# A new emission order for the first third of a fused gated long-convolution and mixer kernel

## The chip, the cores and the metric

The kernel runs on one core of a Trainium2 chip. Its time is the device time of one execution in microseconds (us). Five engines work side by side, each through its own list of instructions in order: TensorE (PE) with matmuls and transposes, VectorE (DVE) and ScalarE (ACT) with element-wise work and with emptying PSUM, GpSimd (POOL) with small work and the gathers of V, and SyncE (SP), which asks for nearly all transfers. Semaphores tie the lists together. Since every list is in order, an instruction that waits holds up all behind it on its engine.

## The reference

```python
x = A_q                                              # 2048 tokens x 640 channels, bf16
g = sigmoid((x * gate_w).sum(-1, keepdims=True))
# a: shifted k times v, then a causal convolution over all 2048 tokens per channel, by FFT
k_shift = sum over t<4 of shift(k, t) * shift_k[:, t];  kv = k_shift * v
y = irfft(rfft(pad(kv)) * rfft(pad(ssm_k)))[:2048] + kv * ssm_D
a = x * y
# b: a token-shift MLP and a second MLP, both with a layernorm ahead and a residual
h  = gelu(layernorm(x) @ w1)                         # 640 x 640
hs = concat(h's four groups of 160 channels, shifted by +1, -1, +2, -2 tokens) @ w2
x1 = x + hs
b  = x1 + gelu(layernorm(x1) @ w3) @ w4              # 640 x 1536, 1536 x 640
out = g * a + (1 - g) * b
```

## The kernel before

The whole program is written as small *steps*, and one string, `ORDER`, lists all 1101 of them. A step is named `what.arguments:number`, for example `mlp1.1.4:0`; the loop `emit` calls them one by one, and each call puts its instructions at the end of the lists of its engines. So the order of every engine is the order of that string, and nothing reorders it. A string of letters among the arguments (`VAAV`) says for each part of a step whether DVE (V) or ACT (A) empties its PSUM tile. A second table, `SLOTS`, gives each temporary its buffer: `c` the eight PSUM banks, `row` four SBUF buffers of 128x2560 that hold K chunks (`kn`), normalised rows (`xn`) and the rows `stg` on their way to DRAM, `gt` and `gq` smaller ones. A buffer is reused when its last reader is done, so a new tile can wait for an emptying, or for a transfer, several steps back.

The tokens are cut as token = 16p + t, with p the partition and t in 0..15 (`NT`), so a chunk `c` of four t's holds 512 tokens. The first third of the program ("the head" below) does this:

- `warm` issues 23 matmuls on zeros. `load_x0`, `load_x`, `k_load:0`, `load_w1`, `load_w2`, `load_h`, `load_gw` ask SP for x, K, W1, W2, the convolution kernel (`E`, `E4`) and the gate's weights; `v_load` asks POOL to gather V.
- `x_stats`, `x_norm`, `x_turn` take the layernorm of chunk c and transpose it. Chunks 0 and 1 are turned on PE (into `xt`), chunks 2 and 3 by a transposing transfer on SP's queue (`x_turn.3.D`, `x_turn.2.D`, line 653; tile `xt`).
- `mlp1.c.u` is one of 20 groups of five matmuls with W1 (tile `WN`; u=4 takes the mixed columns `WM`) and a gelu into `HT`. `h_shift` copies shifted channels of `HT` into `HM` on POOL.
- `k_load` transposes K on PE into `KT`; `k_wrap` and `kv_consts` prepare `KW` and `DG`; `tap.k` (k=0..4) is the 4-tap convolution for 128 channels, 76 small matmuls into four PSUM banks, each then multiplied by V in place in `KV` (line 606 from PSUM, or line 600 on ACT and then 603 on DVE).
- `step1.KV.c` is the first stage of the Fourier transform of `KV`: five pairs of matmuls, ten emptyings into `stg`, two sends to DRAM (`S_x`). `step1.HT0.c` does the same for the convolution kernel, which `h_transpose` has turned (`S_h`).
- `w2.t` multiplies row t of the shifted h by W2 (tile `WP`), adds x on DVE and sums squares on ACT. `z_rows` and `z_cols` are the gate's matmuls; `z_rows:0` spreads the gate's weights (`GWR<-GW`) on POOL. `t2_table` and `i_tables` make the twiddle factors; `t2_table:1` has a POOL instruction of 128x1024 integers (line 322).

After the head come the rest of `w2`, `step1.HT0`, the second MLP (`w3`, line 841; `w4`, line 868), the second and third Fourier stages (`step2`, `product`, `step3`), `step4` and the stores.

Of the kernel before, what the change touches and what calls it, by code (L numbers as in the profile page):

```python
# [41 lines left out]
def kernel(  # L42
# [837 lines left out]
    def step4(t1, ev):  # L880
# [53 lines left out]
        "x_stats.0.VVVA:4 "
        "x_stats.0.VVVA:5 "
        "x_stats.0.VVVA:6 "
        "warm:4 "
        "row_order:0 "
        "k_load.2.VAV:0 "
        "f1_table:0 "  # L940
        "x_norm.0.VVAA:0 "
        "x_norm.0.VVAA:1 "
        "f4_table:1 "
        "x_stats.1.VVVV:0 "
        "k_load.3.AVA:2 "
        "load_x.3:0 "
        "x_norm.0.VVAA:2 "
        "x_stats.1.VVVV:1 "
        "k_load.3.AVA:3 "
        "x_turn.0.AAA:0 "  # L950
        "k_load.3.AVA:6 "
        "k_load.2.VAV:5 "
        "load_w1.1:0 "
        "x_norm.0.VVAA:3 "
        "k_load.2.VAV:1 "
        "x_stats.1.VVVV:2 "
        "x_turn.0.AAA:1 "
        "x_stats.1.VVVV:3 "
        "x_turn.0.AAA:2 "
        "x_stats.1.VVVV:4 "  # L960
        "load_w1.0:0 "
        "x_stats.1.VVVV:5 "
        "x_stats.3.VVAA:0 "
        "k_load.3.AVA:4 "
        "x_norm.1.VVVV:0 "
        "x_turn.0.AAA:4 "
        "k_load.2.VAV:3 "
        "x_turn.0.AAA:3 "
        "x_turn.0.AAA:5 "
        "x_stats.3.VVAA:1 "  # L970
        "x_norm.1.VVVV:1 "
        "x_norm.1.VVVV:2 "
        "v_load.2:0 "
        "k_load.0.AAV:0 "
        "f1_table:1 "
        "mlp1.0.2:0 "
        "mlp1.0.3:0 "
        "x_norm.1.VVVV:3 "
        "v_load.0:0 "
        "k_load.1.AVV:0 "  # L980
        "k_load.2.VAV:6 "
        "mlp1.0.0:0 "
        "load_x.2:0 "
        "x_stats.3.VVAA:2 "
        "x_turn.1.VVV:0 "
        "x_turn.1.VVV:4 "
        "mlp1.0.1:0 "
        "x_stats.3.VVAA:3 "
        "x_turn.1.VVV:1 "
        "k_load.2.VAV:4 "  # L990
        "x_stats.3.VVAA:4 "
        "x_stats.3.VVAA:5 "
        "k_load.0.AAV:3 "
        "x_turn.1.VVV:5 "
        "mlp1.0.3:1 "
        "x_stats.3.VVAA:6 "
        "x_turn.1.VVV:2 "
        "v_load.3:0 "
        "x_turn.1.VVV:3 "
        "k_load.1.AVV:3 "  # L1000
        "w1_mixed:0 "
        "v_load.1:0 "
        "mlp1.0.0:1 "
        "x_stats.2.VVAA:0 "
        "mlp1.0.2:1 "
        "k_load.0.AAV:1 "
        "mlp1.0.1:1 "
        "x_stats.3.VVAA:7 "
        "k_load.0.AAV:5 "
        "mlp1.1.2:0 "  # L1010
        "x_norm.3.VVVV:0 "
        "x_norm.3.VVVV:1 "
        "k_load.0.AAV:4 "
        "load_cj:0 "
        "k_load.0.AAV:2 "
        "mlp1.1.2:1 "
        "x_norm.3.VVVV:2 "
        "x_norm.3.VVVV:3 "
        "x_stats.2.VVAA:1 "
        "k_load.1.AVV:5 "  # L1020
        "mlp1.0.4:0 "
        "k_load.1.AVV:4 "
        "mlp1.0.4:1 "
        "k_load.1.AVV:1 "
        "d_fold:0 "
        "mlp1.1.4:0 "
        "x_turn.3.D:0 "
        "kv_consts:0 "
        "x_stats.2.VVAA:2 "
        "mlp1.1.0:0 "  # L1030
        "k_load.2.VAV:2 "
        "k_wrap:0 "
        "k_load.1.AVV:6 "
        "mlp1.1.4:1 "
        "k_load.0.AAV:6 "
        "x_stats.2.VVAA:3 "
        "t2_table:0 "
        "load_w2:0 "
        "mlp1.1.3:0 "
        "k_load.1.AVV:2 "  # L1040
        "tap.3.VAVA:0 "
        "mlp1.1.0:1 "
        "x_stats.2.VVAA:4 "
        "h_shift.1:0 "
        "mlp1.1.3:1 "
        "tap.4.VAAV:0 "
        "x_stats.2.VVAA:5 "
        "tap.3.VAVA:1 "
        "tap.3.VAVA:3 "
        "tap.3.VAVA:5 "  # L1050
        "h_shift.0:0 "
        "mlp1.1.1:0 "
        "tap.4.VAAV:7 "
        "x_stats.2.VVAA:6 "
        "tap.3.VAVA:4 "
        "tap.4.VAAV:1 "
        "load_h.2:0 "
        "tap.3.VAVA:7 "
        "z_cols:0 "
        "mlp1.1.1:1 "  # L1060
        "load_gw:0 "
        "tap.4.VAAV:5 "
        "tap.4.VAAV:3 "
        "mlp1.3.1:0 "
        "tap.3.VAVA:2 "
        "x_stats.2.VVAA:7 "
        "x_norm.2.AVVV:0 "
        "mlp1.3.1:1 "
        "mlp1.3.4:0 "
        "tap.4.VAAV:2 "  # L1070
        "mlp1.3.0:0 "
        "x_norm.2.AVVV:1 "
        "tap.4.VAAV:8 "
        "x_norm.2.AVVV:2 "
        "x_norm.2.AVVV:3 "
        "h_shift.0:1 "
        "tap.4.VAAV:6 "
        "tap.3.VAVA:6 "
        "mlp1.3.4:1 "
        "tap.4.VAAV:4 "  # L1080
        "mlp1.3.0:1 "
        "tap.2.AVAA:0 "
        "x_turn.2.D:0 "
        "h_shift.3:0 "
        "tap.0.AVAA:0 "
        "tap.2.AVAA:3 "
        "tap.2.AVAA:7 "
        "tap.2.AVAA:5 "
        "tap.3.VAVA:8 "
        "mlp1.3.3:0 "  # L1090
        "tap.0.AVAA:3 "
        "h_shift.0:2 "
        "tap.0.AVAA:5 "
        "tap.2.AVAA:8 "
        "h_shift.3:1 "
        "mlp1.3.2:0 "
        "tap.0.AVAA:4 "
        "tap.2.AVAA:6 "
        "tap.0.AVAA:1 "
        "mlp1.3.3:1 "  # L1100
        "tap.0.AVAA:6 "
        "tap.1.VAVA:0 "
        "tap.0.AVAA:7 "
        "tap.1.VAVA:5 "
        "tap.1.VAVA:1 "
        "tap.2.AVAA:4 "
# [961 lines left out]
```

## Time and profile before

| what | us |
|---|---|
| three timed runs | 226.66, 231.12, 231.19 (median 231.12) |
| the profiled execution | 229.4 |
| its span, first to last instruction | 227.6 |
| busy: PE, DVE, ACT, POOL | 217.3, 185.1, 171.6, 37.8 |

The span is 1.8 us shorter than the execution's own time, for what lies before the first and after the last instruction. PE is busy for 95% of the span, and the profile counts an instruction as busy from its start to its modelled end, so the gaps that are left are few; they lie mostly in the first 45 us. The granted TensorE clock is 1.00 throughout.

### The profile page before, as it was taken

Reading aid. Unit: us, or ns where it says so; the run is one execution under the profiler, and the core shown is the slowest. Engines: PE = TensorE matmul, PEld = TensorE weight load, DVE = VectorE, ACT = ScalarE, POOL = GpSimd, SP = SyncE. Lnnn points to the kernel's source line nnn. Section 1 sums busy time; section 2 is a strip of 40 time slices with the busy share of each in tenths; the row PEclk is TensorE's granted clock in tenths of the full one; section 3 lists DMA queues with packets and bytes.
Section 4 is the critical chain, followed back from the end, with each engine's and each line's share of the span. In section 5 each row is a group of like instructions: output and inputs, shape, how many; then the busy total and the mean of one; then the engine's idle time right before and its main releaser. Section 6 shows DMA issues by size and latency. Waiting matters only on the chain.

```text
span 227.6 us, 6057 instructions
## 1 busy us (share of the span) xinstructions
PE 217.3 (95%) x2428; PEld 121.4 (53%) x2428; DVE 185.1 (81%) x447; ACT 171.6 (75%) x341; POOL 37.8 (17%) x91
## 2 busy tenths in 40 slices
PE   8989988799999997999999999999999999999994
PEld 3647545337855553334665544555533547657762
DVE  7999996977889968981899997989999941439994
ACT  4999986869899978999987597976989450266450
POOL 4247247806000331300510000000000000000000
PEclk9999999999999999999999999999999999999999
DMA  6999999888999899997799590593694779418915
GB/s 247 398 386 306 265 259 162 256 340 292 384 350 411 285 206 287 347 397 232 252 147 370 134 260 17 127 334 121 78 313 172 234 264 365 196 29 322 319 75 183
DMA packets 41802, 57.61 MB, mean 253 GB/s; under 512 B 18478, under 2 KB 34478, under 8 KB 41518
## 3 DMA queue, kind: packets, MB, share of 16 engines
q1 hardware_dynamic: 41198, 54.60, 76.8%
q0 software_dynamic: 576, 2.62, 3.3%
q8 instruction: 19, 0.31, 0.6%
q14 instruction: 9, 0.07, 0.1%
HBM read 34.93 MB, written 18.35 MB: 234 GB/s over the span
## 4 chain that ended last, share of the span: by engine, by line
PE 73%; ACT 14%; DMA 6%; DVE 4%; issue 1%; ACTq 0%
PE ps L868 23%; PE ps L841 22%; PE psm L708 5%; PE psw L789 5%; PE ps L466 4%; PE ps L894 4%; ACT stg L361 4%; DMA S_h<-stg 3%; PE ps L513 3%; PE ps L424 2%; ACT HT L711 2%; PE pst L391 2%; DMA S_x<-stg 2%; ACT KT L361 1%; PE psk L591 1%
## 5 line engine op out<-in xcount | busy, mean ns | idle before, releaser
L841 PE MATMUL ps<-x1t,W 128*128 128x512 bf16 x240 | 56.1, 380 | 0.1
L868 PEld LDWEIGHTS <-gt 128*128 128x128 bf16 x384 | 36.2, 98 | 17.8 <-issue 3.0
L845 ACT ACTIVATE gt<-ps 128x512 bf16<-128x512 f32 x48 | 27.6, 609 | 19.0 <-PE ps L868 10.6
L841 PEld LDWEIGHTS <-W 128*128 128x128 bf16 x240 | 21.8, 98 | 28.2 <-issue 5.5
L361 ACT CAST stg<-ps 128x512 bf16<-128x512 f32 x55 | 28.8, 608 | 5.3 <-PE ps L424 3.4
L868 PE MATMUL ps<-W4a,gt 128*128 128x320 bf16 (+2 forms) x160 | 27.1, 300 | 0.0
L868 PE MATMUL ps<-W4b,gt 128*128 128x320 bf16 (+2 forms) x160 | 27.0, 300 | 0.0
L871 DVE SCALAR_TENSOR_TENSOR X<-ps,OMG,X 128x320 bf16<-128x320 f32 (+2 forms) x32 | 17.2, 547 | 11.9 <-PE ps L868 11.7
L789 PE MATMUL psw<-WP,HT 128*128 128x320 bf16 x116 | 21.4, 300 | 1.3 <-ACT stg L361 1.3
L361 ACT CAST gs<-ps 128x320 bf16<-128x320 f32 x41 | 15.6, 440 | 8.8 <-PE ps L513 4.8
L708 PE MATMUL psm<-xt,WN 128*128 128x512 bf16 x80 | 19.1, 380 | 1.8 <-ACT xt L361 0.9
L363 DVE CAST XS<-ps 128x512 bf16<-128x512 f32 x19 | 12.5, 685 | 6.9 <-PE ps L466 6.9
L363 DVE CAST stg<-ps 128x512 bf16<-128x512 f32 x25 | 15.9, 684 | 2.1 <-PE ps L424 2.1
L361 ACT CAST hs<-ps 128x512 bf16<-128x512 f32 x28 | 15.0, 605 | 1.4 <-PE ps L466 1.4
L792 DVE SCALAR_TENSOR_TENSOR X<-psw,X 128x320 bf16<-128x320 f32 x32 | 14.5, 487 | 1.7 <-PE psw L789 1.5
L789 PEld LDWEIGHTS <-HT 128*128 128x128 bf16 x116 | 10.7, 98 | 8.1 <-issue 4.4
L898 ACT ACTIVATE y<-ps,GS 128x320 bf16<-128x320 f32 x22 | 10.4, 526 | 5.7 <-PE ps L894 3.5
L711 ACT ACTIVATE HT<-psm 128x512 bf16<-128x512 f32 x20 | 11.9, 616 | 3.1 <-PE psm L708 2.9
L868 PE MATMUL ps<-W4c,gt 128*128 128x320 bf16 (+2 forms) x64 | 13.9, 299 | 0.0
L708 PEld LDWEIGHTS <-WN 128*128 128x128 bf16 x80 | 7.5, 97 | 10.7 <-issue 1.3
L363 DVE CAST gs<-ps 128x320 bf16<-128x320 f32 x23 | 10.7, 485 | 2.4 <-PE ps L513 1.7
L789 PE MATMUL psw<-WP,HM 128*128 128x320 bf16 x44 | 12.3, 299 | 0.0
(155 smaller groups left out, 378.1 us busy)
## 6 DMA issues: line engine op xcount, KB each, us to landing
S_x<-stg SPq DMA_DIRECT2D x8, 640.0 KB, 4.3
S_h<-stg SPq DMA_DIRECT2D x8, 640.0 KB, 6.5
ax<-S_x SPq DMA_DIRECT2D x8, 640.0 KB, 7.8
ax<-S_h SPq DMA_DIRECT2D x8, 640.0 KB, 5.8
S_g<-gs SPq DMA_DIRECT2D x8, 640.0 KB, 3.5
kn<-in_A_k_dram SPq DMA_DIRECT2D x4, 640.0 KB, 5.0
E<-in_A_ssm_k_dram SPq DMA_DIRECT2D x5, 512.0 KB, 7.0
q<-in_A_q_dram SPq DMA_DIRECT2D x4, 640.0 KB, 4.6
```

Source lines behind the costliest of these rows:

```text
L361: A.copy(out=dst, in_=src)
L363: V.tensor_copy(out=dst, in_=src)
L466: PE.matmul(ps[j][q:q + 32, lo - 512 * u:hi - 512 * u], lhsT=CMP[HALF[j], 8 * b + 4 * h + i, c, :], rhs=st[name, 2 * b + h][HALF[j], i, lo ...
L708: PE.matmul(ps[:].rearrange("p (a b) -> p a b", a=4), lhsT=W1N[:, k, 160 * u:160 * u + P] if u < 4 else W1M[:, k, :], rhs=xt[:, :, k, :], ...
L711: A.activation(out=st["HT"][:, 4 * c:4 * c + 4, u, :], in_=ps[:].rearrange("p (t b) -> p t b", t=4), func=ACT.Gelu_apprx_tanh)
L789: PE.matmul(ps[:], lhsT=h_tile(f, t1), rhs=W2P[:, f, o:o + W], start=(f == 0), stop=(f == 4))
L792: V.scalar_tensor_tensor(out=X1[:, t1, o:o + W], in0=box["ps"][:], scalar=1.0, in1=X[:, t1, o:o + W], op0=ALU.mult, op1=ALU.add, accum_out ...
L841: PE.matmul(ps[:].rearrange("p (a b) -> p a b", a=4), lhsT=st["W3"][:, k, f * P:(f + 1) * P], rhs=xt[:, :, k, :], start=(k == 0), stop=(k ...
L845: A.activation(out=st["gt", c, f // 4][:, f % 4, :], in_=ps[:], func=ACT.Gelu_apprx_tanh)
L868: PE.matmul(ps[:], lhsT=st["gt", c, f // 4][:, f % 4, i * P:(i + 1) * P], rhs=st["W4", f // DC][:, f % DC, o:o + w], start=(f == 0), stop= ...
L871: V.scalar_tensor_tensor(out=X1[:, t1, o:o + w], in0=box["ps"][:], scalar=OMG[:, t1:t1 + 1], in1=X1[:, t1, o:o + w], op0=ALU.mult, op1=ALU ...
L898: A.activation(out=box["y"][:], in_=box["ps"][:], func=ACT.Copy, scale=GS[:, t1:t1 + 1])
```

## The change

The first 341 names of `ORDER` are written anew; from `w2.1:2` on (entry 341, counted from 0) the string is the same, except for one argument: `step1.KV.0` has other emptying letters. Every step of the head is still there once. What differs is their order, the letters (`tap.0` is `VVVA` and was `AVAA`, for example), and `SLOTS`, whose rows `c`, `row`, `gt` and `gq` are written anew for the whole program. Two places of the diff:

```diff
     SLOTS = {
-        "c": "012345670124703510347205142356401723605162370514731057423671045261304732641374153670421350627413"
+        "c": "012345670567401372605436057243610723014763024167503642167304521673251607426013572460157234603521"
...
-        "row": "01230213021302320123012031203120310310303",
+        "row": "01230123012323103210321302130213023023030",
...
     ORDER = (
-        "open.L1.left:0 "
-        "open.A2.right:0 "
-        "consts0:0 "
-        "load_x0.0:0 "
-        "warm:0 "
...
+        "open.L1.left:0 open.A2.right:0 consts0:0 warm:0 warm:1 warm:2 warm:3 warm:4 load_x0.0:0 consts0:1 "
...
+        "h_shift.1:0 h_shift.1:1 h_shift.1:2 load_w2:0 x_norm.3.VVVV:0 h_shift.1:3 x_norm.3.VVVV:1 x_norm.3.VVVV:2 "
+        "x_norm.3.VVVV:3 x_stats.2.VVAA:0 x_stats.2.VVAA:1 x_stats.2.VVAA:2 x_turn.3.D:0 x_stats.2.VVAA:3 "
+        "load_h.3:0 x_stats.2.VVAA:4 x_stats.2.VVAA:5 tap.4.VAAV:7 load_h.0:0 mlp1.1.3:0 tap.3.VVVA:7 tap.3.VVVA:6 "
```

SP's list of transfers, from the eighth entry on, before (`DMA_TRANSPOSE` are `x_turn.3` and `x_turn.2`, `WP` is W2, `E` the convolution kernel, `E_1123` its last 128 channels, `S_x<-stg` the sends of `step1.KV`):

```order
L564 DMA kn<-in_A_k_dram 128x2560 x2
L190 DMA X<-in_A_q_dram 128x2560
...
L653 DMA_TRANSPOSE xt_506<-xn 128x20x128
L207 DMA WP<-in_B_w_dram 128x4x640
L208 DMA WP<-in_B_w_dram 128x1x640
L183 DMA E<-in_A_ssm_k_dram 128x2048
L200 DMA GW<-in_gate_w_dram 128x5x1
L653 DMA_TRANSPOSE xt_506<-xn 128x20x128
L183 DMA E<-in_A_ssm_k_dram 128x2048 x2
L187 DMA E_1123<-in_A_ssm_k_dram 128x2048
L187 DMA E_1123<-in_A_ssm_k_dram 128x2032
L183 DMA E<-in_A_ssm_k_dram 128x2048
```

and the same stretch after the change:

```order
L190 DMA X<-in_A_q_dram 128x2560
L207 DMA WP<-in_B_w_dram 128x4x640
L208 DMA WP<-in_B_w_dram 128x1x640
L653 DMA_TRANSPOSE xt_701<-xn 128x20x128
L183 DMA E<-in_A_ssm_k_dram 128x2048 x3
...
L653 DMA_TRANSPOSE xt_701<-xn 128x20x128
L187 DMA E_1032<-in_A_ssm_k_dram 128x2048
L187 DMA E_1032<-in_A_ssm_k_dram 128x2032
L200 DMA GW<-in_gate_w_dram 128x5x1
L183 DMA E<-in_A_ssm_k_dram 128x2048
L438 DMA S_x<-stg 128x2560 x2
```

W2 has moved ahead of the first transposing transfer; three rows of `E` stand between the two transposing transfers, where W2, one row of `E` and the gate's weights stood; the last three rows and the gate's weights now come right ahead of the first sends.

DVE's list just ahead of and behind `x_norm.3` (the four `xn` in a row), before:

```order
L686 BN_STATS b_435<-X 128x6 x2
L687 BN_AGGR mv<-b_435 128x2
L665 TENSOR_SCALAR xn<-X,RS,NB 128x640 x4
L363 COPY KT<-pst 128x1024
L553 TENSOR_REDUCE i_509<-IDB 128x32
L554 TENSOR_TENSOR DG<-i_509,cr 128x640
L363 COPY KT<-pst 128x1024
L571 MEMSET KW 128x15
L572 COPY KW<-KT 128x15x64
L573 COPY KW<-KT 128x15x63
```

and after:

```order
L571 MEMSET KW 128x15
L572 COPY KW<-KT 128x15x64
L573 COPY KW<-KT 128x15x63
L363 COPY xt<-pst 128x512
L363 COPY xt<-pst 128x1024
L553 TENSOR_REDUCE i_494<-IDB 128x32
L554 TENSOR_TENSOR DG<-i_494,cr 128x640
L665 TENSOR_SCALAR xn<-X,RS,NB 128x640 x4
L686 BN_STATS b_694<-X 128x6 x2
L687 BN_AGGR mv<-b_694 128x2
L606 TENSOR_TENSOR KV<-psk,KV 128x16x32 x4
```

The preparation for the taps (`KW`, `DG`) has moved ahead of `x_norm.3`, and a pair of statistics of chunk 2 behind it.

On PE, all 23 warm matmuls now come first, where they were dealt out among the first K transposes; the first MLP's groups begin after 76 transposes of K and x instead of 60; the taps come one at a time with one to three `mlp1` groups between them (4, 3, 2, 1, 0), where two pairs (3 with 4, 2 with 0) and then tap 1 stood; and two halves of `w2` (rows 2 and 1) come before the gate's `z_rows`. `t2_table:1` moves from the last tap to a place behind the h_transposes.

More of the change, by code (lines that the diff above doesn't have):

```diff
@@ L934 @@
[L934 to L1106, printed above, removed]
-        "mlp1.3.2:1 "
-        "load_h.1:0 "
-        "mlp1.2.2:0 "
-        "tap.0.AVAA:8 "
-        "tap.2.AVAA:1 "
-        "tap.1.VAVA:7 "
-        "h_shift.1:1 "
-        "tap.0.AVAA:2 "
-        "load_h.3:0 "
```

926 lines of the change are left out of this document (6 added, 920 removed), and 165 rows, old and new, of the table ORDER.

## The prediction

> **What bounds the kernel now.** I read the windows first, cut where the new order ends. Columns are the stretch in us, its length, and the busy time of each engine with its count.
>
> ```profile
> 0.00:25.00 25.00, 22.85 (x180) 13.45 (x181) 22.58 (x87) 21.57 (x37) 10.32 (x25) 1.00 0.94 338
> 25.00:45.00 20.00, 17.03 (x432) 9.44 (x431) 17.88 (x46) 16.66 (x33) 13.16 (x31) 1.00 0.95 219
> 45.00:65.00 20.00, 19.54 (x190) 12.38 (x190) 16.14 (x39) 15.99 (x28) 3.62 (x7) 1.00 0.90 331
> 65.00:85.00 20.00, 20.00 (x147) 11.57 (x146) 16.70 (x58) 18.57 (x40) 4.18 (x8) 1.00 1.09 321
> 97.00:227.00 130.00, 127.26 (x1385) 69.97 (x1383) 100.95 (x190) 87.78 (x186) 3.70 (x11) 1.00 0.69 216
> ```
>
> The first number behind the length is PE: it is full from 65 us to the end but for a few us. In the first 65 us it is busy for 22.85 + 17.03 + 19.54 = 59.4 us, so it idles 5.6 us. That is all a new head can win directly, since PE's work in the head does not change. Then PE's waits up to 100 us (total, times, longest), and the chain of work that ended last around the place where the two orders meet:
>
> ```profile
> PE ps L424 <- DVE KV L603: 1.5, 1, 1.5
> PE psw L789 <- ACT stg L361: 1.3, 1, 1.3
> PE psz L229 <- DVE NPI L249: 1.0, 1, 1.0
> PE psm L708 <- ACT xt L361: 0.9, 1, 0.9
> PE psk L591 <- issue: 0.8, 1, 0.8
> ```
> ```profile
> 66.79 1.46 PE psw L789 x10
> 68.25 0.75 PE ps L424 x6
> ```
>
> The ten matmuls at 66.79 are `w2.1:2` and `w2.11:0`, the first of the kept order. I call 66.79 the meeting point. Behind it every engine does the same work in the same order, so I let a shift of the meeting point pass to the end one for one. The sum is then an account of PE's gaps before that point: those of the new order against 5.6 us.
>
> **What goes.** The 1.5 us wait is the last tap. Here DVE and POOL stand in each other's way:
>
> ```profile
> 43.12 1.91 POOL L322 TENSOR_TENSOR n<-ab 128x1024 int32<-128x1024 int32 x1
> 43.31 2.00 DVE L603 TENSOR_TENSOR KV<-yk,KV 128x512 bf16<-128x512 bf16 x1
> L603 DVE TENSOR_TENSOR KV<-yk,KV x12: 409/485/1997, 30.3 to 43.3; 128x512 bf16<-128x512 bf16 x12
> ```
>
> A product of the same shape takes 0.41 us at the least (the last row: shortest, median and longest of the twelve, in ns); it took 2.00 beside POOL's 1.91. In the new order that POOL instruction runs beside casts from PSUM, long after the taps, so this wait goes, and with it the 0.8 and 0.9 us ones, whose places no longer exist. All are inside the 5.6.
>
> **What comes, 1: the opening.** Warm matmuls first:
>
> ```profile
> 0.98 6.73 PE L229 MATMUL psz<-WZ 128*128 128x512 bf16 x20 [0.98 <-DVE NPI L249]
> 8.24 0.81 PE L229 MATMUL psz<-WZ 128*128 128x512 bf16 x3
> 6.29 1.28 ACT L278 ACT_TABLE_LOAD   x1
> 8.70 0.20 POOL L659 TENSOR_TENSOR NB<-MU,RS 128x4 f32<-128x4 f32 x1
> 10.40 0.93 ACT L663 ACTIVATE xn<-X,NB,RS 128x640 bf16<-128x640 bf16 x1
> ```
>
> 20 in 6.6 us and 3 in 0.6, so PE is free at 8.2 and turns K chunk 1 (20 transposes) until 9.4. `x_turn.0` now waits for ACT: three of the four rows are normalised there (`AAAV`), 0.82 us each from about 8.95, when POOL has the scale (8.70 and 0.20), as before. Row 1 is there at 10.6, row 2 at 11.4. With K transposes between, PE loses about 1.4 us; with the start 2.4. Bounds 0.5 (ACT drops a table load it had at 6.29 and may be earlier) to 2.0.
>
> **What comes, 2: the first transposing transfer.** Prices of PE's groups, from the chain: 12 transposes 0.67, three `mlp1` 3.40, a tap 1.09, 48 transposes of `E` 3.17, three pairs of `step1` 0.75.
>
> ```profile
> 16.86 0.67 PE pst L620 x12
> 31.67 3.40 PE psm L708 x15
> 40.26 1.09 PE psk L591 x76
> 58.33 3.17 PE pst L391 x48
> 57.57 0.75 PE ps L424 x6
> ```
>
> Up to `mlp1.3.4`, the first user of chunk 3, the new list has the warm-up (to 8.2), 120 transposes (7.0, at 0.67 for 12 as K's are), 10 `mlp1` (11.3), 3 taps (3.3) and the 1.4 above: PE arrives at 31.2. The data wait for `x_norm.3` on DVE, then for the transfer:
>
> ```profile
> 22.07 1.52 DVE L665 TENSOR_SCALAR xn<-X,RS,NB 128x640 bf16<-128x640 bf16 x4 [0.19 <-POOL NB L659]
> 24.10 0.36 DVE L553 TENSOR_REDUCE i<-IDB 128x32 bf16<-128x128 bf16 x1
> 24.49 0.83 DVE L554 TENSOR_TENSOR DG<-i,cr 128x640 bf16<-128x640 bf16 x1
> 25.86 0.41 DVE L572 COPY KW<-KT 128x960 bf16<-128x960 bf16 x1
> 26.18 0.80 DVE L573 COPY KW<-KT 128x945 bf16<-128x945 bf16 x1
> 23.61 4.46 SPq L653 DMA_TRANSPOSE xt<-xn  x1
> 34.04 3.98 SPq L653 DMA_TRANSPOSE xt<-xn  x1
> DMA to landing us min/median/max: 8.0/8.0/8.0
> ```
>
> DVE is busy almost throughout the first 25 us, so what is put ahead of `x_norm.3` delays it: `DG` (24.10 to 25.25: 1.15), `KW` (25.86 to 26.91: 1.05), two K copies of 1024 and one of 512 (0.6 and 0.35 each as they follow one another); taken away are a pair of statistics (1.0), one normalised row (1.52 for four: 0.4) and 0.25 of x copies. Net +2.1, less the 0.19 idle: end at 25.5 instead of 23.6. The landing of 8.0 us makes 33.5, a wait of 2.3. Bounds: 1.7 if DVE loses no time at hand-offs, 2.9 if W2's 0.8 MB, now ahead of V's gather, holds the rings 0.6 us longer. The early W2 itself gains nothing: its first user was at 52.25 and would be at about 48.
>
> **What comes, 3: the second one.** `x_norm.2` ends on DVE at about 34.4 (four tap products, the statistics and a pair of scales more ahead, fewer behind), much as before (34.04). From 33.5, PE has five `mlp1`, two taps and five pairs, 9.1 us, and wants chunk 2 at 42.6; 34.4 + 8.0 = 42.4 would do. But three rows of `E`, 1.57 MB, stand ahead in SP's queue, asked for behind the first transposing transfer. That what is asked for later lands later on this queue shows in a tiny one:
>
> ```profile
> 29.99 0.82 SPq L200 DMA_DIRECT2D GW<-in_gate_w_dram  x1
> GW<-in_gate_w_dram SPq DMA_DIRECT2D x1, 1.2 KB, 7.1
> 25.00:30.00 5.00, 4.57 (x163) 2.93 (x162) 4.86 (x20) 5.00 (x12) 1.55 (x3) 1.00 1.12 197
> 30.00:35.00 5.00, 4.37 (x20) 1.67 (x18) 4.97 (x14) 3.68 (x7) 2.95 (x8) 1.00 0.86 245
> 35.00:40.00 5.00, 4.23 (x163) 2.84 (x162) 3.22 (x7) 3.53 (x7) 4.08 (x14) 1.00 1.00 177
> ```
>
> 1.2 KB needed 7.1 us, to 37.1, behind W2 and a row of `E`; the transposing transfer behind it landed at 42.0, 4.9 us on. At 245 GB/s (last column, the stretch in which plain loads moved) three rows take 6.4 us from 33.5, and 4.9 more make 44.8: a wait of 2.2. At 197 it is 3.8; if the rings share freely, 0. I take 2.2, the stretch with the same kind of load.
>
> [...]
>
> **What comes, 4: sends of `KV`.** `step1.KV.2` reuses the buffers of `KV.1`, so its emptyings wait until those rows have landed:
>
> ```profile
> 49.35 4.28 DMA S_x<-stg
> 53.71 3.03 ACT L361 CAST stg<-ps 128x512 bf16<-128x512 f32 x6 [0.21 <-DMA S_x<-stg]
> ```
>
> Before, this cost ACT 0.21 us. In the new order the last three rows of `E` and the gate's weights, 1.56 MB, are asked for just ahead. From 44.8 they take 4.7 us at the 331 GB/s of the third window, the two sends 2.0 each: landed at 53.5, cast at 54.0. PE reaches `KV.2:6`, which needs those two banks, at 44.8 + 7.9 = 52.7. A wait of 1.3; bounds 0.2 (as before) and 2.7 (at the 219 GB/s of the second window).
>
> The two `w2` halves ahead of `z_rows` need `HM` from POOL by 48 and it is there by 43; their cost is nothing as long as POOL is that far ahead, else up to 1 us. `SLOTS` I cost at nothing: the banks I followed were all emptied before their next user came, but for those named.
>
> **Sum.** 2.4 + 2.3 + 2.2 + 1.3 = 8.2 against 5.6: 2.6 us later at the meeting point. On the profiled execution, 227.6 of span and 1.8 around it, that is 229.4 + 2.6 = **232.0 us**, 1.1% more; beside the median of the runs shown (231.12, of which the profiled one is 1.7 under) it is 0.4% more. 2% is about what a measurement of this kernel can tell from no change. By the bounds: 1.5 + 1.7 + 0 + 0.2 = 3.4 gives 227.2; 3.0 + 2.9 + 3.8 + 2.7 = 12.4 gives 236.2.
>
> **Rivals.**
>
> *Faster.* No transfer is late: the rings take the rows of `E` in time and the gaps are the 3.4 of the lower bounds, a gain of 2.2. ACT reaches the meeting point less loaded (one table load of 1.28 fewer), its sends of `HT0` start earlier, and the 1.3 us wait of `w2` for `stg` in the second list goes too: 229.4 - 3.5 = 225.9. For it: the losses of before have named causes and the new order removes them. Against: 34.4 + 8.0 has 0.2 us to spare, and any backlog uses that up. 0.26.
>
> *Slower.* The queue of SP runs at the pace that a transposing transfer leaves it, 177 GB/s. Three rows then take 8.9 us, chunk 2 lands at 47.3 (wait 4.7), and the rows behind it move the sends to about 59, where PE wants them at 55.2: with the casts a wait of 4.8. Gaps 2.4 + 2.3 + 4.7 + 4.8 = 14.2, 8.6 more than before; half a us may be regained at 85: 237.5. It decides below some 200 GB/s. For it: the 35 to 40 row; against: 331 GB/s in the next window. 0.32.
>
> *Nothing happens.* The gaps change place and stay 5.6: 229.4. It needs both transposing transfers at or below 2 us of wait and free sends. 0.08.
>
> The forecast has 0.34, and its own range is 227.2 to 236.2. Faster by over 2% has 0.26, within 2% 0.42 (the forecast and the rival in which nothing happens), slower by over 2% 0.32. The range, reaching into both other cases, is 224.5 to 238.5.
>
> **What would show it.** In the new profile: one tap product of 2.00 us gone; PE waiting near 31 us for `mlp1.3.4` by 2.3, near 43 us for `mlp1.2.4` by about 2, near 53 us in `step1.KV.2` for casts that wait for `S_x`; the landing of the second transposing transfer over 10 us; `w2.1:2` at 69.4. It is wrong if the second `xt` lands within 8 us, if PE is the last to arrive at chunk 3, or if the shift at 69 is not the shift at the end.

## The result, and the profile after

| kernel | median us | runs | range us |
|---|---|---|---|
| before | 227.5 | 8 | 226.66 to 231.19 |
| after the change | 232.63 | 8 | 232.15 to 233.38 |

The ratio is 1.0242, with a 95% interval of 1.022 to 1.0264: the new order is 2.4% slower. It counts only fast runs: two of the eight of before (231.12 and 231.19) are slow ones, and the median of the other six is 227.1. The time lies in the predicted range and 0.6 us above the predicted 232.0, but "within 2%", which had the most chance, did not happen. Two numbers have to be kept apart. The profiled execution of before took 229.4 us, 1.9 more than the median of its eight runs; that of after took 232.64, its median. So the two traces show 3.3 us (spans 227.6 and 230.9) of the 5.1 between the medians. What the quicker executions of before do better is not shown.

The windows of after, cut as those of before (PE's busy time is the first number behind the length):

```profile
0.00:25.00 25.00, 21.13 (x169) 12.39 (x170) 20.93 (x84) 19.61 (x32) 10.44 (x25) 1.00 0.92 311
25.00:45.00 20.00, 17.67 (x433) 9.69 (x432) 17.30 (x39) 16.38 (x33) 11.90 (x30) 1.00 0.92 248
45.00:65.00 20.00, 18.43 (x162) 9.87 (x159) 15.41 (x35) 15.17 (x27) 5.16 (x7) 1.00 0.78 265
97.00:227.00 130.00, 129.99 (x1438) 71.13 (x1438) 102.96 (x196) 91.01 (x193) 5.89 (x18) 1.00 0.69 219
```

PE idles 3.9 us in the first window (2.2 before) and 1.6 in the third (0.5 before). The last transposes of `E` and the meeting point `w2.1:2`, in PE's timeline of after:

```profile
65.78 1.24 PE L391 MATMUL pst<-IDB,E 128*128 128x128 bf16 x16
70.93 0.43 PE L789 MATMUL psw<-WP,HT 128*128 128x320 bf16 x2
```

The meeting point is at 70.93 in this view. In the same view of before it is at 66.72 (the chain in the prediction has 66.79), so it is 4.2 later. At the end 3.3 are left: the wait of 1.3 us of `w2` for `stg` near 85 us has gone. The seven largest of PE's waits of after up to 100 us:

```profile
PE pst L620 <- DMA kn<-in_A_k_dram: 1.6, 1, 1.6
PE ps L424 <- ACT stg L361: 1.3, 1, 1.3
PE psz L229 <- DVE NPI L249: 1.0, 1, 1.0
PE psm L708 <- DVE KV L606: 0.8, 1, 0.8
PE pst L620 <- ACT xn L663: 0.7, 2, 0.4
PE psk L591 <- ACT yk L600: 0.7, 1, 0.7
PE psk L591 <- DVE KV L606: 0.4, 1, 0.4
```

There is no wait for `xt<-xn`, the transposing transfers, on which 4.5 us of my sum rested. Instead there are waits for the tap products (`KV`, `yk`), which I had not named at all. The chain of work that ended last says why:

```profile
2.58 9.31 DMA X<-in_A_q_dram
...
16.38 1.02 POOL RS L658
...
22.02 9.53 DMA KV<-in_A_v_dram,ROWS
...
31.70 0.51 POOL HM L762
...
36.80 1.07 POOL RS L658
...
38.17 1.24 DVE xn L665 x3
...
50.94 4.83 DMA S_x<-stg
```

Read from the top: x's chunk 1, now fifth in SP's list, lands at 11.9; its statistics keep DVE until 16.3; POOL forms its scale at 16.38 and only behind that asks for V, from 17.87 to 22.02; the last V lands at 31.6. The gathers in before and in after (issue, count, duration, first and last start; then issue to landing):

```profile
L173 POOL DMA_INDIRECT KV<-in_A_v_dram,ROWS x4: 937/938/1220, 15.6 to 19.7; - x4
DMA to landing us min/median/max: 6.4/6.8/7.6
```
```profile
L173 POOL DMA_INDIRECT KV<-in_A_v_dram,ROWS x4: 937/1012/1221, 17.9 to 22.0; - x4
DMA to landing us min/median/max: 8.9/9.1/9.5
```

V is asked for 2.4 us later and needs 1.9 more: 31.6 instead of 27.3. Before, that left 3 us until the first tap product at 30.3. Now DVE and POOL both start at the landing:

```profile
31.68 2.48 DVE L606 TENSOR_TENSOR KV<-psk,KV 128x512 bf16<-128x512 f32 x4 [2.32 <-PE psm L708]
31.70 0.49 POOL L762 COPY HM<-HT 32x384 bf16<-32x384 bf16 x1 [4.91 <-DMA KV<-in_A_v_dram,ROWS]
34.22 0.38 PE L591 MATMUL psk<-DG,KT 32*128 32x128 bf16 x13 [0.37 <-DVE KV L606]
37.48 0.62 PE L591 MATMUL psk<-DG,KT 32*128 32x128 bf16 x16
41.27 0.38 PE L591 MATMUL psk<-DG,KT 32*128 32x128 bf16 x13 [0.67 <-ACT yk L600]
```

DVE's wait is put down to PE's matmul of that moment, but POOL's copy beside it names the gathers, and the second profile below names them for DVE too. From there to 45.9 DVE works off the products of the taps, with statistics, scales and normalised rows between them and one pause of 0.25 us, and the last three taps on PE wait for their banks: from their first to their last instruction they take 1.68, 1.30 and 2.26 us, 5.2 together where the tap of before shown above took 1.09, so 2.0 too much. Only half of that appears as waits (0.37 and 0.67). The rest is inside rows counted as busy, like the one at 37.48, whose sixteen matmuls took 0.40 in an unhindered tap.

### The profile page after: what moved, and what is told of

It reads as the page before. It is cut to its first block, busy times and chain, and to the rows that moved or that the text cites. A ratio compares the mean times of both kernels' runs of the same rounds, so it can differ in the third digit from the quotient of the medians.

```text
span 230.9 us, 6058 instructions
## 1 busy us (share of the span) xinstructions
PE 219.6 (95%) x2428; PEld 121.6 (53%) x2428; DVE 185.3 (80%) x447; ACT 172.0 (75%) x337; POOL 38.2 (17%) x91
## 4 chain that ended last, share of the span: by engine, by line
PE 71%; DMA 10%; DVE 8%; POOL 5%; issue 2%; ACT 1%; SPq 1%; POOLq 0%; ACTq 0%; DVEq 0%
PE ps L841 23%; PE ps L868 23%; PE psw L789 6%; PE ps L466 5%; DMA KV<-in_A_v_dram,ROWS 4%; DMA X<-in_A_q_dram 4%; PE ps L894 4%; PE ps L424 3%; PE ps L513 3%; PE pst L391 2%; DVE X L792 2%; DMA S_x<-stg 2%; POOL HM L762 2%; PE psm L708 1%; POOL KV L173 1%
## 5 line engine op out<-in xcount | busy, mean ns | idle before, releaser
L841 PEld LDWEIGHTS <-W 128*128 128x128 bf16 x240 | 21.9, 98 | 28.6 <-issue 5.9
L361 ACT CAST stg<-ps 128x512 bf16<-128x512 f32 x50 | 27.0, 597 | 5.0 <-PE ps L424 2.7
L871 DVE SCALAR_TENSOR_TENSOR X<-ps,OMG,X 128x320 bf16<-128x320 f32 (+2 forms) x32 | 17.2, 548 | 11.9 <-PE ps L868 11.7
L363 DVE CAST stg<-ps 128x512 bf16<-128x512 f32 x30 | 19.2, 683 | 3.0 <-PE ps L424 2.9
L708 PEld LDWEIGHTS <-WN 128*128 128x128 bf16 x80 | 7.3, 97 | 11.9 <-issue 4.4
L363 DVE CAST gs<-ps 128x320 bf16<-128x320 f32 x23 | 10.7, 484 | 2.4 <-PE ps L513 1.7
L798 ACT ACTIVATE jk<-X 128x640 bf16<-128x640 bf16 x16 | 12.1, 757 | 0.5 <-DVE X L792 0.4
```

Of the source, the lines that this page charges most:

```text
L361: A.copy(out=dst, in_=src)
L363: V.tensor_copy(out=dst, in_=src)
L708: PE.matmul(ps[:].rearrange("p (a b) -> p a b", a=4), lhsT=W1N[:, k, 160 * u:160 * u + P] if u < 4 else W1M[:, k, :], rhs=xt[:, :, k, :], ...
L798: A.activation(out=jk[:], in_=X1[:, t1, :], func=ACT.Square, accum_out=S12[:, 1, t1:t1 + 1])
L841: PE.matmul(ps[:].rearrange("p (a b) -> p a b", a=4), lhsT=st["W3"][:, k, f * P:(f + 1) * P], rhs=xt[:, :, k, :], start=(k == 0), stop=(k ...
L871: V.scalar_tensor_tensor(out=X1[:, t1, o:o + w], in0=box["ps"][:], scalar=OMG[:, t1:t1 + 1], in1=X1[:, t1, o:o + w], op0=ALU.mult, op1=ALU ...
```

## The experiments

All times are medians in us. The kernel before ran in every call too, and its own median moved between calls (226.98 to 228.9). So two kernels are compared by their ratios within one call, and the mechanism by the traces. The ratio is the middle of its interval, not the quotient of the two medians beside it.

| kernel | us | before in that call | ratio | 95% interval |
|---|---|---|---|---|
| after_again | 232.04 | 226.98 | 1.022 | 1.0192 to 1.0248 |
| x3_dve | 233.13 | 226.98 | 1.0264 | 1.0232 to 1.0296 |
| before_w2_early | 233.48 | 226.98 | 1.0294 | 1.0268 to 1.0321 |
| v_first | 236.11 | 228.9 | 1.0278 | 1.0197 to 1.036 |
| w2_back | 232.05 | 228.9 | 1.0143 | 1.0063 to 1.0223 |
| e_back | 236.31 | 228.9 | 1.032 | 1.0248 to 1.0392 |
| x3_last | 232.01 | 228.9 | 1.0127 | 1.0057 to 1.0196 |
| opening | 232.75 | 228.45 | 1.0153 | 1.0066 to 1.024 |
| sx_free | 231.74 | 228.45 | 1.0131 | 1.0052 to 1.0211 |
| combo | 237.19 | 228.45 | 1.0357 | 1.0275 to 1.0439 |
| before_x3_first | 229.72 | 228.45 | 1.0032 | 0.9998 to 1.0065 |
| before_t2_late | 228.41 | 228.48 | 1.001 | 0.9979 to 1.0041 |

One thing stays open for the single repairs w2_back, x3_last, opening and sx_free. By ratio (1.0127 to 1.0153) they lie 0.7 to 1.2 points under the changed kernel (1.022 and 1.0242). By median (231.74 to 232.75) they lie within 0.9 us of it (232.04 and 232.63). The changed kernel was not run in their calls. These were on chip 3, where before took 228.45 and 228.9; after_again was on chip 5, where it took 226.98. So it isn't shown whether the repairs gained or before was only slower there.

### The changed kernel again

> The changed kernel as it is, in one call with the next two, so that they stand against it on one chip and not only against the kernel before. Its ratio was 1.024; the runs of single repairs lay at 1.013 to 1.015 although their traces reach the meeting point no sooner. If the ratio belongs to the change, 1.022 to 1.026 again; if the chip matters, 1.013 to 1.018. The wait for the first K chunk at 9 us, there in two of three profiles of this opening, is expected at 1.4 to 1.8 us.

It measured 1.022: the loss is there in this call too. In the profile mlp1 starts at 16.02, 0.66 us sooner than in the first one, and yet the last transposes of `E` end at 67.02 in both. The reason is in DVE's timeline:

```profile
31.64 1.89 DVE L606 TENSOR_TENSOR KV<-psk,KV 128x512 bf16<-128x512 f32 x3 [2.93 <-DMA KV<-in_A_v_dram,ROWS]
```

The first product waits 2.9 us for V and starts where it started before. So those 0.66 us of PE's opening made no difference between these two executions, in which the first product came at the same time.

### W2 back behind the first transposing transfer

```diff
-h_shift.1:2 load_w2:0 x_norm.3.VVVV:0
+h_shift.1:2 x_norm.3.VVVV:0
...
-x_turn.3.D:0 x_stats.2.VVAA:3
+x_turn.3.D:0 load_w2:0 x_stats.2.VVAA:3
```

> The changed kernel with the request for W2 moved back behind the first transposing transfer, where the kernel before has it. Theory W2 EARLY (0.8 MB ahead of V on the rings is what makes V late): V lands 2.3 us sooner (0.8 MB at 345 GB/s), the first tap product starts at about 29.5 us instead of 31.68, time 231 or less. INPUTS: V is late mostly because POOL asks late (17.9 against 15.6), W2 is worth at most 1 us of landing, time 232 to 232.6. E ROWS: the rows of E move back behind W2, so chunk 2's transposing transfer is as late as before or later: 232.6 or more.

The landing of V fell to a median of 7.0 us (9.1), and the first product came at 29.26:

```profile
29.26 2.48 DVE L606 TENSOR_TENSOR KV<-psk,KV 128x512 bf16<-128x512 f32 x4 [1.42 <-DMA KV<-in_A_v_dram,ROWS]
63.69 1.23 PE L391 MATMUL pst<-IDB,E 128*128 128x128 bf16 x16
```

`E` ends 2.1 us sooner, as the product starts 2.4 sooner. But this is the quickest of four executions (230.58 to 233.23), and in it V was asked for 1.6 us sooner too, because the first loads happened to land earlier (x in at most 7.7 us, for 9.3 in the changed kernel). From the last request to the first product it is 8.9 us here and 9.7, 10.3, 9.5, 10.1 and 10.3 in the five profiles of the changed order with W2 early (after, after_again, e_back, sx_free, opening): early W2 went with 0.7 to 1.4 us more for V's landing. Combo, which also has W2 back, agrees: its V landed in 6.5 to 7.2 us. The median is that of the changed kernel, the ratio is 1.0143; whether the time got shorter is not settled. The expected 231 or less was missed (232.05).

### The opening

```diff
-load_x.3:0 k_load.1.AVV:0 x_stats.0.VVVA:3
+k_load.1.AVV:0 load_x.3:0 x_stats.0.VVVA:3
...
-x_stats.3.VVAA:0 k_load.1.AVV:1 x_stats.3.VVAA:1 x_stats.3.VVAA:2 k_load.1.AVV:5 x_stats.3.VVAA:3 x_stats.3.VVAA:4
+k_load.1.AVV:1 k_load.1.AVV:5
...
-x_norm.0.AAAV:3 x_turn.0.AAV:4
+x_norm.0.AAAV:3 x_stats.3.VVAA:0 x_stats.3.VVAA:1 x_stats.3.VVAA:2 x_stats.3.VVAA:3 x_stats.3.VVAA:4 x_turn.0.AAV:4
```

> The changed kernel (ratio to the kernel before 1.024) with K chunk 1 asked for ahead of x's chunk 3, and chunk 3's first statistics on ACT and DVE moved behind the normalising of chunk 0. Theory OPENING (PE's start is late because K chunk 1 is fourth in SP's list, and because ACT waits for chunk 3 before it normalises chunk 0): no wait for K at 9 us (1.59 us in the changed kernel), ACT's three normalised rows end near 11.5 us (13.8), the first mlp1 starts when W1 is there, at 15 to 16.3 (16.7): 0.5 to 1.5 us gained, ratio 1.018 to 1.022. Rival BYTES (W1 stands behind six other loads, nothing else matters): mlp1 still starts with W1's landing at 16.2 or later, ratio 1.024.

The median shows no gain (232.75), while the ratio (1.0153) is even under the 1.018 that OPENING allowed. The profile is of the slowest of four executions (231.61 to 233.75). In it the wait moved from K chunk 1 (0.63 left) to K chunk 3, in PE's timeline:

```profile
13.63 0.40 PE L620 MATMUL pst<-IDB,kn 128*128 128x128 bf16 x4 [2.25 <-DMA kn<-in_A_k_dram]
```

and x's chunk 1 came later, so that the last V was asked for at 22.50; the first product waited for it until 32.76 and `E` ended at 68.13. mlp1 starts at 17.49, where BYTES said 16.2 or later. By the trace BYTES is nearer than OPENING: W1 landed 11.8 and 12.3 us after its requests, for 11.6 and 12.1 in the changed kernel. Its ratio of 1.024 did not come.

### V first

```diff
-x_stats.0.VVVA:6 x_norm.0.AAAV:0
+x_stats.0.VVVA:6 kv_alloc:0 v_load.1:0 v_load.3:0 v_load.0:0 v_load.2:0 x_norm.0.AAAV:0
...
-x_stats.1.VVVV:5 kv_alloc:0 v_load.1:0
+x_stats.1.VVVV:5
...
```

> The changed kernel (232.63 us), with POOL asking for V right behind the scale of chunk 0 instead of behind the scale of chunk 1 (x_stats.1), so at about 9 to 14 us instead of 17.9 to 22. Theory INPUTS (the order in which the first inputs arrive is what costs: chunk 1's statistics hold up V on POOL, V is late for the taps): the last V lands at 27 us or earlier (31.6 in the changed kernel), DVE's first tap product starts near 29.5 instead of 31.68, PE's waits for KV products near 32 and 34 us go, and the time falls by 1 to 2 us, to 231. Rival RINGS: 2.6 MB of V now compete with K chunks 3 and 2 and with W1; W1 lands 2 us or more after 17.3, the first mlp1 starts after 18 us (16.7), and the time stays at 232.6 or rises. Rival E ROWS (my forecast's cause, plain rows ahead of the transposing transfers): no change but for noise, 232.6.

The rival was right, and stronger than I had it. V is asked for at 9.1 to 13.2 and no tap waits for it, but W1 now lands beside it after 18.7 us (11.6 to 12.1 in the changed kernel):

```profile
23.35 5.66 PE L708 MATMUL psm<-xt,WN 128*128 128x512 bf16 x15 [6.21 <-DMA WN<-in_B_w_dram]
```

PE waits 6.2 us, and the fifteen matmuls, 3.40 in the changed kernel, take 5.66, at a granted clock of 0.61 and 0.71 in the two windows from 20 to 30 us. The time is 7.2 us over the kernel before of its call, where the changed kernel lies 5.1 over. Asking for V at this place, ahead of all else on POOL, is no repair.

### Chunk 3 of x behind W1

```diff
-load_x.3:0 k_load.1.AVV:0 x_stats.0.VVVA:3
+k_load.1.AVV:0 x_stats.0.VVVA:3
...
-k_load.2.AVA:0 k_load.3.AVA:1
+k_load.2.AVA:0 load_w1.0:0 load_w1.1:0 load_x.3:0 k_load.3.AVA:1
...
-x_stats.3.VVAA:5
+x_stats.3.VVAA:0 x_stats.3.VVAA:1 x_stats.3.VVAA:2 x_stats.3.VVAA:3 x_stats.3.VVAA:4 x_stats.3.VVAA:5
...
```

> The changed kernel with x's chunk 3 asked for behind W1 instead of third, W1 asked for right behind the K chunks, and chunk 3's statistics on DVE and ACT moved behind the emptyings of chunk 0. INPUTS: K chunk 1 lands at 7 us (10.3), ACT normalises chunk 0 from 8.95 us (11.3, since it no longer waits for chunk 3's rows), x chunk 1 lands at 10 (11.9), W1 at 14.5 to 15.5 (17.3), the first mlp1 starts near 14.7 (16.7), V is asked for at 15.7 (17.9): 2 us or more gained, 230 to 231. RINGS (the bytes ahead of mlp1 count, not their order) : 0.66 MB fewer ahead of W1 are worth 1.7 us by 385 GB/s, but chunk 3's statistics now stand ahead of the first gelus on ACT and cost up to 2.6 us there: 232 to 233. E ROWS: the head gains, but PE then waits for the transposing transfers: 232 or more, with waits for xt near 31 and 44 us.

Every expected landing came: no wait for K, mlp1 at 14.38, the last V asked for at 19.33, DVE waiting for PE at the first tap product and not for V. The time is still 232.01, as RINGS had it, and the ratio is 1.0127. PE's timeline:

```profile
20.48 1.29 PE L620 MATMUL pst<-IDB,xn 128*128 128x128 bf16 x16 [1.62 <-ACT jk L682]
23.53 2.33 PE L708 MATMUL psm<-xt,WM 128*128 128x512 bf16 x5
```

The statistics of chunk 3 now stand in front of the first gelus on ACT: a wait of 1.62, and behind it five matmuls that take 2.33 us instead of 1.24, at a granted clock of 0.76 between 20 and 25 us. V was taken off the path and ACT took most of its place: in this trace `E` ends at 66.10, 0.9 sooner than the 67.02 of the changed kernel.

In x3_dve chunk 3's statistics are all on DVE (the six steps of `VVVV` for the eight of `VVAA`):

```diff
-x_stats.3.VVAA:0 x_stats.3.VVAA:1 x_stats.3.VVAA:2 x_stats.3.VVAA:3 x_stats.3.VVAA:4 x_stats.3.VVAA:5
+x_stats.3.VVVV:0 x_stats.3.VVVV:1
...
-x_stats.3.VVAA:6
+x_stats.3.VVVV:2 x_stats.3.VVVV:3 x_stats.3.VVVV:4
```

> As x3_last (x's chunk 3 asked for behind W1), and all of chunk 3's statistics on DVE, so that ACT does none in front of the first gelus; the values are the same. INPUTS (bytes that nobody needs yet stand ahead of K and W1; the late start and the late V are the whole loss but for the 1.3 us of the sends): no wait over 0.5 us on PE before the sends, the first mlp1 at 14.4 (16.7), the last transposes of E end at 63 to 64 (67.0 in the changed kernel, 62.7 before, where two fewer steps of w2 stand in front), time 3 to 4 us under the changed kernel on the same chip. Rival ACT (the new order has as much to do for ACT and DVE before 25 us as they can take, whatever the order of inputs): the 1.6 us that x3_last lost at 20 us come back as waits for DVE's copies, and the time stays within 1 us of the changed kernel.

It is no faster than the changed kernel of the same call (1.0264 against 1.022). PE waited 1.92 for K chunk 0 at 19.8 and 1.29 for DVE's normalised rows at 21.9. The second wait is what rival ACT describes, with DVE in ACT's part. The first and larger one is for a load, asked for at 12.32 and 7.4 us on its way, that neither theory named.

### The rows of E, the sends, and all repairs at once

e_back moves the three rows of `E` that stood between the transposing transfers:

```diff
-x_stats.2.VVAA:3 load_h.3:0 x_stats.2.VVAA:4
+x_stats.2.VVAA:3 x_stats.2.VVAA:4
...
-tap.4.VAAV:7 load_h.0:0 mlp1.1.3:0
+tap.4.VAAV:7 mlp1.1.3:0
...
-x_stats.2.VVAA:7 load_h.1:0 tap.1.AVVA:5
+x_stats.2.VVAA:7 tap.1.AVVA:5
...
-x_turn.2.D:0 tap.4.VAAV:2
+x_turn.2.D:0 load_h.3:0 load_h.0:0 load_h.1:0 tap.4.VAAV:2
```

> The changed kernel with the three rows of E that stand between the two transposing transfers moved behind the second one. E ROWS (my forecast's term of 2.2 us): the second transposing transfer lands sooner and PE gains up to 2 us near 43 us: 230.5. INPUTS: that transfer was in time anyway (landed at 44.4, wanted at 46.9), so nothing is gained there; the rows of E now stand ahead of the sends of KV, whose landing slips by up to 3 us (1 MB at 330 GB/s), and PE's wait of 1.3 us near 56 grows: 232.6 to 234.5.

Slower, as INPUTS expected, and by more. PE's timeline near 55 us:

```profile
56.95 0.37 PE L424 MATMUL ps<-KV,F 64*128 64x512 bf16 x1 [2.60 <-ACT stg L361]
58.49 0.37 PE L424 MATMUL ps<-KV,F 64*128 64x512 bf16 x1 [1.17 <-ACT stg L361]
```

All rows of `E`, 3 MB, stand ahead of the sends here. ACT's casts waited 3.50 and 0.96 us for the sends, where the changed kernel had one such wait of 1.76. So here rows ahead went with late sends, as my forecast had it. The same term looked at from the other side is sx_free, which takes the plain rows away from right ahead of the sends:

```diff
-load_h.1:0 tap.1.AVVA:5
+load_h.1:0 load_gw:0 load_h.2:0 tap.1.AVVA:5
...
-step1.KV.1.AAAVAVVAVA:15 h_shift.3:0
+step1.KV.1.AAAVAVVAVA:15 load_h.4:0 h_shift.3:0
```

> The changed kernel with the last row of E and the gate's weights asked for ahead of the second transposing transfer, and the two rows of E4 behind the first sends of KV. Theory SENDS (the plain rows ahead of the sends make their landing late, the 1.3 us term of my forecast): the first sends land in 2.5 to 3.5 us (4.8), PE's wait of 1.28 us for stg in step1.KV.2 falls below 0.3, and the time falls by 1 us: ratio 1.019 to 1.020. Rival E ROWS: two more small loads ahead of the second transposing transfer make it 1.5 us later (46 instead of 44.4), still in time at 46.9; if transposing transfers stand behind plain rows as I had it, PE then waits for xt near 47 by 1 us or more and nothing is gained: 1.024.

```profile
56.84 0.37 PE L424 MATMUL ps<-KV,F 64*128 64x512 bf16 x1 [1.50 <-ACT stg L361]
```

The wait stayed (1.50 for 1.28): the first send took 3.0 us, as in the changed kernel, and the second still 5.0. So rows right ahead are not needed for this wait. What makes the second send slow stays open: here the last two rows of `E` are asked for right behind the sends, at 51.49 and 52.40, while the second is under way, and no run has the sends alone. For comparison, the two sends took 3.8 and 4.3 us in the kernel before, and 3.0 to 3.6 in before_w2_early.

combo makes three repairs at once, those of opening, w2_back and sx_free:

> The changed kernel with three repairs together: the opening (K chunk 1 ahead of x's chunk 3, chunk 0 normalised ahead of chunk 3's statistics), W2's request behind the first transposing transfer, and the sends of KV freed of the plain rows ahead. INPUTS: their parts add up, 0.5 to 1.5 for the opening, 0.5 to 1 for W2, 1 for the sends: 2 to 3.5 us off, ratio 1.009 to 1.015; what is left is W1 behind one K chunk more. E ROWS: the second transposing transfer now stands behind W2, four rows of E and the gate's weights, 2.9 MB; if it waits for them it lands near 48 and PE waits 2 us or more for it: ratio 1.02.

It is the slowest (1.0357), and here my forecast's mechanism did show. `x_turn.2.D` is asked for at 39.20 behind W2, four rows of `E` and the gate's weights, asked for since 31.4:

```profile
48.95 1.07 ACT L361 CAST stg<-ps 128x512 bf16<-128x512 f32 x2 [4.07 <-DMA xt<-xn]
49.71 0.58 PE L424 MATMUL ps<-KV,F 64*128 64x512 bf16 x1 [4.40 <-DVE stg L363]
50.23 2.31 PE L708 MATMUL psm<-xt,WM 128*128 128x512 bf16 x5
```

It lands 9.7 us later (4.9 in the changed kernel). The first to suffer is not `mlp1` but `stg`: its row buffer is that of the normalised chunk 2, which the transfer still reads, so ACT and DVE can't cast, and PE waits 4.4 us.

### Parts of the change alone, in the kernel before

before_x3_first:

```diff
-k_load.3.AVA:0 f4_table:0
+load_x.3:0 k_load.3.AVA:0 f4_table:0
...
-k_load.3.AVA:2 load_x.3:0 x_norm.0.VVAA:2
+k_load.3.AVA:2 x_norm.0.VVAA:2
```

> The kernel before, with one thing of the change alone: x's chunk 3 asked for third, ahead of the first K chunk and of chunk 1 (0.66 MB that nobody needs yet). OPENING: K chunk 3 lands 1.7 us later (7.8 instead of 6.1) and x chunk 1 too (about 10.5), V is asked for up to 1.5 us later than 15.6, and mlp1 starts up to 1.5 us later than 13.2: ratio 1.004 to 1.007. Rival BYTES: the bytes ahead of W1 are the same, W1 lands as before and mlp1 starts at 13.2: ratio 1.000.

1.0032, interval 0.9998 to 1.0065: between the two theories. mlp1 starts 1.1 us later (14.28 for 13.19) and V is asked for 0.5 us later, less than the 1.5 expected. At most 0.65% of the time: a small part of 2.4%.

before_w2_early:

```diff
-load_x.2:0 x_stats.3.VVAA:2
+load_x.2:0 load_w2:0 x_stats.3.VVAA:2
...
-t2_table:0 load_w2:0 mlp1.1.3:0
+t2_table:0 mlp1.1.3:0
```

> The kernel before, with W2 alone asked for early, right behind the last chunk of x. W2 EARLY: V lands up to 2.3 us later than 27.3, still ahead of the first tap product at 30.3, and x's chunk 3 by its transposing transfer no later: ratio 1.000; the price of early W2 shows only where V is late already. E ROWS: the gate's weights and a row of E no longer stand behind W2, the second transposing transfer lands sooner than 42.0, and PE's 0.6 to 1 us near 37 to 42 go: ratio 0.996. Against both: if V's landing slips by over 3 us, the taps wait and the ratio is 1.004 or more.

1.0294. A ratio of 1.004 or more was expected if V slipped by over 3 us, and V did land at 30.5, 3.2 later. But the loss is far above that, and it comes by a load that no expectation looked at. I had put W2 ahead of the 5 KB of tap coefficients `cr` (`load_cj`):

```profile
L543 SPq DMA_DIRECT2D cr<-in_A_shift_k_dram x1: 1391/1391/1391, 14.5 to 14.5; - x1
...
DMA to landing us min/median/max: 16.2/16.2/16.2
```

They land at 30.7; DVE stands for 6.2 us before `DG`, PE for 4.4 before the taps. The change itself asks for `cr` (14.86) ahead of W2 (16.09), where `DG` never waited. So this run doesn't price the change's early W2. It prices a place: with W2 one entry ahead of `cr` the kernel took 6.5 us more.

before_t2_late takes the gain that I had counted on:

```diff
-w2.15:0 t2_table:1 step1.KV.2.AVAVAVAAAA:4
+w2.15:0 step1.KV.2.AVAVAVAAAA:4
...
-h_shift.2:0 step1.KV.2.AVAVAVAAAA:9
+h_shift.2:0 t2_table:1 step1.KV.2.AVAVAVAAAA:9
```

> The kernel before, with one part of the change alone that my forecast counted as a gain: the 128x1024 integer sum on POOL (t2_table:1) moved from the last tap to behind the first copy of h_shift.2, so to about 52.6 us. CLASH (POOL's sum beside DVE's last tap product is what stretches that product to 2.00 us): the product takes 0.42 to 0.6 us, PE's wait of 1.49 us at 45 us goes, and the end comes 1.0 to 1.5 us sooner: ratio 0.9935 to 0.9955. Rival HIDDEN (behind that wait PE runs into the emptying of the first Fourier stage, which is bound by ACT and DVE and gives the time back): ratio 0.998 to 1.000. Rival OTHER CLASH (the sum now runs beside DVE's additions of x behind w2, which read SBUF too, and stretches one of those by up to 1.5 us): PE waits for psw near 54 us and nothing is gained.

```profile
L603 DVE TENSOR_TENSOR KV<-yk,KV x12: 410/436/825, 31.9 to 44.6; 128x512 bf16<-128x512 bf16 x12
```

The longest product is 0.83 us for 2.00, the clash and PE's wait of 1.49 are gone, and the time is the same: 1.001, 0.9979 to 1.0041. HIDDEN is nearest by the time: the interval leaves room for a gain of at most 0.5 us. The trace shows it only in part. It is of an execution of 229.95, 1.5 above its median, whose last tap ended 1.3 later than that of before (42.58 and 41.28) by other waits, of 1.42 and 1.23. Behind the last tap the casts of the first Fourier stage start 1.4 us sooner; 0.7 of that is given back by the last transposes of `E`, 0.5 of it to a wait for ACT's casts at 55 us, and the other 0.7 stays to the end. No version tried is faster than the kernel before.

## Why the prediction was right and where not

- **The opening (2.4).** Under-sized: 0.98 + 1.59 + 0.72 + 0.29 = 3.6 us. That is more than the upper bound of 3.0. The failing step is "three of the four rows are normalised there", with a start "from about 8.95". ACT had three statistics of chunk 3 in front of them and waited 2.61 us for that chunk:

```profile
8.85 0.74 ACT L680 ACTIVATE jk<-X 128x640 bf16<-128x640 bf16 x1 [2.61 <-DMA X<-in_A_q_dram]
11.31 2.53 ACT L663 ACTIVATE xn<-X,NB,RS 128x640 bf16<-128x640 bf16 x3
```

  I had read the letters and not the list of loads: K chunk 1, which I took as there at 8.2, is fourth in it.
- **The first transposing transfer (2.3): nothing.** It landed at 33.8 (27.36 and 6.4), near my 33.5, but by luck: `x_norm.3` ended at 27.3 and not at 25.5, and the landing took 6.4 and not 8.0. PE came for it at 35.2 and not at 31.2. Of these 4.0, 1.2 are the opening, 0.6 the warm-up (to 8.77, not 8.2), 1.1 waits for tap products, 0.2 a wait for a gelu, and the rest rows that ran longer than I priced them. The step "three taps (3.3)" assumed that V is there. I had the issue of V and the place of W2 in front of me and gave V's delay no term.
- **The second one (2.2): nothing.** It was asked for at 39.5 (34.4 in the sum), since POOL's scale of chunk 2 stands behind a copy that waits for V; the rows of `E`, asked for between 31.7 and 33.2, landed 4.2, 6.0 and 6.8 us after their requests, the last at 39.6, and it took 4.9:

```profile
L653 SPq DMA_TRANSPOSE xt<-xn x2: 3082/3704/4326, 27.4 to 39.5; - x2
...
DMA to landing us min/median/max: 4.9/5.7/6.4
```

  So next to nothing of the rows of `E` was under way ahead of the tile. In combo more was, and what was asked for later did land later: the gate's weights, asked for at 35.42, landed at 44.4, and the tile, asked for at 39.20, at 48.9.
- **The sends (1.3): 1.28**, where it was said, as waits of `step1.KV.2` for `S_x`. The size held. The reason, rows of `E` right ahead, is not borne out: in sx_free they are gone and the wait is 1.50. Whether rows behind the sends take their place there is open. My upper bound was also wrong: 1.56 MB at 219 GB/s take 7.1 us, which makes 3.7 and not 2.7, and 237.2 for the upper end of the sum instead of 236.2.
- **What goes.** The 2.00 us product is gone, as said. That its 1.5 us would be a gain is not borne out by before_t2_late.
- **The shift passes one to one.** 4.2 at the meeting point, 3.3 at the end. The 0.9 that came back are less than the wait near 85 that is gone (1.3), which was a sentence of the "faster" rival.
- **The sum.** Two things were mixed in it. Up to the meeting point, PE's windows are these, before and after:

```profile
0.00:66.72 66.72, 61.14 (x812) 36.06 (x813) 57.74 (x175) 55.93 (x100) 27.11 (x62) 1.00 0.93 301
0.00:70.93 70.93, 63.16 (x812) 36.18 (x813) 59.19 (x175) 56.47 (x96) 27.49 (x62) 1.00 0.89 286
```

  PE idled 5.6 us before and 7.8 after, where I had 8.2. That came near by exchange, which is luck: 4.5 us that did not exist (the two transposing transfers), against 2.4 of waits for tap products (0.75, 0.37, 0.67, 0.35 and 0.29), 1.2 more in the opening and 0.2 for a gelu. The other 2.0 of the shift of 4.2 come from a step that failed: "PE's work in the head does not change". The same 812 matmuls are busy for 63.16 us instead of 61.14. Part of that stands in the taps (6.31 for 5.71) and in `step1.KV` (6.06 for 5.65), whose rows are longer than before; most of it I have not traced. A small slip: 120 transposes at 0.67 for 12 make 6.7, not 7.0.
- **The base.** 232.0 was built on the profiled 229.4. On the median of before, 227.5, the same 2.6 would have given 230.1, 2.5 too little.
- **The signs.** Two of the six came: the 2.00 us product is gone, and `step1.KV.2` waits 1.28 for `S_x` (near 56, not 53). PE did not wait for `xt` near 31 and 43, the second landing took 4.9 and not over 10, and `w2.1:2` is at 70.93, not 69.4. All three signs of being wrong came: the second `xt` landed within 8 us, PE was the last to arrive at chunk 3 (35.2, the tile at 33.8), and the shift at the meeting point is not that at the end. So the time lies in the range while the mechanism of 4.5 of the 8.2 us did not occur.

What is shown: in the changed kernel the taps start when V lands, and PE follows them. From the first tap product to the end of `E`'s transposes it is 35.3, 35.4, 35.7, 35.6 and 35.4 us (after, after_again, w2_back, sx_free, opening), whether mlp1 starts at 15.1 or at 17.5. Where V is in time (x3_last, x3_dve, v_first), ACT, DVE, K or W1 hold PE instead. But V's landing is the smaller part of the shift of 4.2. The first product comes only 1.4 later than before (31.68 for 30.27), with as much PE work done by then (27.8 and 27.7 us). From there to the meeting point it takes 39.3 us instead of 36.5, 2.8 more, the waits behind the first product among them. w2_back's profile agrees: its first product is 1.0 us sooner than that of before (29.26), and its span is still 228.8 for 227.6. Which part of the new order makes these 2.8 us no run has separated, and so it is open how the 5.1 us between the medians divide among the single moves.

## What to carry to other kernels

Follow every load that a step needs back to what its issuing engine does just before: here V hung on the statistics of a chunk of x, and that chunk's load had moved from fourth to fifth place in another engine's list. An account of the waits alone is not enough either: of 4.2 us, 2.0 stood in rows counted as busy. When a head has several bounds within a microsecond or two, one repair moves the wait and does not remove it; price a removed wait by the next one behind it. A small late load can cost more than a large one: 5 KB of coefficients behind W2 went with 6.5 us.
